# A slot dictionary in 32 bits on another queue, smaller constants, and merged weight transfers in a kernel of sliding-window attention and soft mixture of experts

## Chip, cores and metric

The kernel runs on one core of a Trainium2 chip. The metric is the time on the device in microseconds (us), lower is better; a kernel's time is the median of several runs. One run is also recorded by the hardware profiler, which gives the profile and the trace.

## What is computed

Attention over 8 batches, 8 heads, 576 positions and head size 64. Heads 0 to 3 see the last 32 positions, heads 4 to 7 every fourth of the last 128. The result, 4608 rows of 512, goes into a soft mixture of 8 experts with 4 slots each.

```python
scores = (1/8) * q @ k.T                      # per batch and head
rel = pos[:, None] - pos[None, :]
plain   = (rel >= 0) & (rel < 32)                      # heads 0-3
dilated = (rel >= 0) & (rel < 128) & (rel % 4 == 0)    # heads 4-7
attn = softmax(where(mask, scores, -1e9)) @ v
x = attn as [4608, 512]
logits = x @ phi                              # phi: [512, 32], the slot dictionary
slot_input = softmax(logits, axis=0).T @ x    # 32 slots of 512
h = relu(slot_input[e] @ w1[e])               # w1: [8, 512, 1024]
slot_out[e] = h @ w2[e]                       # w2: [8, 1024, 512]
out = softmax(logits, axis=1) @ slot_out
```

All inputs and the output are 32-bit floats; the kernel computes in 16 bits and accumulates in 32.

## The kernel before

**Engines and queues.** TensorE (PE, with its weight loads as PEld) multiplies, VectorE (DVE) and ScalarE (ACT) do elementwise work, GpSimd (POOL) does nothing but issue transfers, SyncE (SP) issues one. A transfer that POOL issues may convert 32 to 16 bits on the way, and nearly all do: q, k, v, phi and the weights come in so, and the output leaves from 16-bit tiles as 32 bits. All transfers run on the same 16 DMA engines. POOL's instructions stand in a fixed order, so a transfer that must wait holds back those behind it; those already issued queue on the DMA engines and are served in order. A transfer waits, besides its data, for the completion of an earlier one: completions are counted by eight semaphores in turn, so the ninth waits for the first.

**Loads.** For each batch `load_raw` (L184) brings Q, K and V as 128 rows of 2304 elements each, into two buffers per kind (raw). The order at the start is Q0, K0, V0, Q1, K1, phi (L459), V1; SP brings the constants `cst` (L449): the mask of the band, two masks for the last rows, an identity `ident`, a repeated small identity `spread`, and `quad`, 548 columns in all. Later `loads` (L514) brings Q, K or V of batch b + 2 as soon as batch b's buffer has been transposed, and from batch 3 on one more weight transfer with each V, the remaining early ones with the last (`load_weights`). `load_w1` brings one expert's w1 as 2 rows of 2048 per partition, `load_w2` one expert's w2 as one row of 4096. When batch 7 has been transposed (L536) the raw buffers are released, and w2_3, w2_4 and w2_5 are loaded in their place; w2_6 and w2_7 go into two slabs that held Q and K, in column halves, first the left halves of both, then the right, each half in two transfers of 4 rows of 256 (L207).

**Attention.** An order written out by hand (`ORDER`, L48) says in which sequence the steps of each batch stand and in which round each falls; it is followed literally. QT, KT and VT (L218) are transposes on VectorE out of the raw buffers. S0 to S2 (L260) are the scores in three groups, E0 to E2 (L269) their exponentials on ScalarE, MK0 to MK2 (L280) the masks on VectorE. VA to VD and their copies (L234, L240) turn V into rows with the help of `ident`. A, R and M (L303, L315, L324, L328) are products with V, reciprocals of the sums and normalisation into xp and xd. XP and XD transpose x (L344 to L351), LG multiplies it with `phi4` (L381, L389), ET (L399) keeps the exponentials, and U sums up the slots' inputs (L428, L442). `phi4` is phi four times side by side; VectorE copies it at the end of the first round (L549), between VT of batch 0 and the first mask.

**Experts.** After the last batch: row sums `rs` with `quad` (L566), the slots' inputs divided and transposed (L574 to L587), `hps` (L597) against all w1, a relu, transposes (L607), hTm (L609, L612). Then `so` (L628): one run of 32 matmuls over w2_0 to w2_3 (row chunk by row chunk, the four experts within each), eight over w2_4, eight over w2_5, then eight each over the left halves of w2_6 and w2_7. `gather_so` (L639) and `spread_so` (L644, L645, with `spread`) make so_sb of the left half, and the output of batches 0 to 5 is computed for its left columns (`emit_fin`: f L651, om L660 on ScalarE and L664 on VectorE in turn) and stored (L673), with the right halves of w2_6 and w2_7 in between; then their right columns, then batches 6 and 7 whole, then the last 64 rows of all batches (om_l, L700). The om tiles take the places of w1_0 to w1_7.

Of the kernel before, what the change touches and what calls it, by code (L numbers as in the profile page):

```python
# [19 lines left out]
WINDOW = 32  # L20
# [4 lines left out]
DMODEL = H * D  # L25
E_EXP = 8
S_PER_E = 4
N_SLOTS = 32
FDIM = 1024
# [6 lines left out]
PW = 160  # L36
LEFT = S - 512
# [24 lines left out]
def piece_w(kind, i):  # L62
    return LEFT if (kind, i) == ("P", 4) else WIDTH[kind]
# [16 lines left out]
def make_consts():  # L80

    a = np.arange(128)[:, None]
    rel = np.arange(PW)[None, :] - a
    band = (rel >= 0) & (rel < WINDOW)
    parts = [band]
    for first in LKEY:
        rel = 512 + np.arange(LEFT)[None, :] - first - a
        seen = LKEY[0] if first < LKEY[0] else S
        parts.append((rel >= 0) & (rel < WINDOW * DIL) & (rel % DIL == 0) & (first + a < seen))
    parts.append(a == np.arange(128)[None, :])  # L90
    parts.append((a % 32) == (np.arange(128)[None, :] % 32))
# [5 lines left out]
def kernel(  # L97
# [18 lines left out]
    o = PW + 2 * LEFT  # L116
    band, lmask = cst[:, 0:PW], [cst[:, PW + LEFT * i : PW + LEFT * i + LEFT] for i in range(2)]
    ident = cst[:, o : o + 128]
    spread = cst[:, o + 128 : o + 256]
    quad = cst[:, o + 256 : o + 260]  # L120
# [9 lines left out]
    so_part = consts.tile([128, DMODEL], FP16, name="so_part")  # L130
# [5 lines left out]
    w1t = [w1_pool.tile([128, 4, FDIM], FP16, name=f"w1_{e}", tag=f"w1_{e}") for e in range(E_EXP)]  # L136
    w2t = {e: w2a_pool.tile([128, 8, DMODEL], FP16, name=f"w2_{e}", tag=f"w2_{e}") for e in range(3)}


    fix = tc.alloc_tile_pool(name="fix", bufs=1)  # L140
# [50 lines left out]

    def load_w1(e):
        nc.gpsimd.dma_start(
            out=w1t[e].rearrange("p (u c) f -> p u (c f)", u=2),
            in_=moe_w1[e].rearrange("(u p c) f -> p u (c f)", u=2, p=128),
        )

    def load_w2(e, s=None):
        src = moe_w2[e].rearrange("(p c) n -> p c n", p=128)
        if s is None:  # L200
            nc.gpsimd.dma_start(
                out=w2t[e].rearrange("p c n -> p (c n)"), in_=src.rearrange("p c n -> p (c n)")
            )
            return
        cols = slice(DH * s, DH * s + DH)
        for u in range(2):
            nc.gpsimd.dma_start(out=w2t[e][:, 4 * u : 4 * u + 4, cols], in_=src[:, 4 * u : 4 * u + 4, cols])  # L207


    def turn(which, b, half):  # L210
# [245 lines left out]
    load_raw("V", 0)  # L456
    for which in "QK":
        load_raw(which, 1)
    nc.gpsimd.dma_start(  # L459
        out=phi_raw.rearrange("p (u c) s -> p u (c s)", u=2),  # L460
        in_=moe_phi.rearrange("(u p c) s -> p u (c s)", u=2, c=2),
    )
# [5 lines left out]
    weights = [(1, e) for e in range(8)] + [(2, e) for e in range(3)]  # L468

    def load_weights(n):  # L470
        for _ in range(n):
            which, e = weights.pop(0)
            (load_w1 if which == 1 else load_w2)(e)

    tmp = {}

# [49 lines left out]
    w2b_pool = None  # L526
    for it in range(B + max(s for _, s in STEPS)):
        for op, stage in STEPS:
            b = it - stage
            if not 0 <= b < B:  # L530
                continue
            step(op, b)
            if op in frees and b + 2 < B:
                loads(frees[op], b + 2)
            left.discard((op, b))
            if w2b_pool is None and not left:  # L536
                raw_pool.release()
                w2b_pool = tc.alloc_tile_pool(name="w2b", bufs=1, side="right")
                for e in (3, 4, 5):
                    w2t[e] = w2b_pool.tile([128, 8, DMODEL], FP16, name=f"w2_{e}", tag=f"w2_{e}")  # L540
                slab_weights(6, "qk0", QK_SLAB)
                slab_weights(7, "qk1", QK_SLAB)
                for e in (3, 4, 5):
# [48 lines left out]
    for fc in range(2):  # L592
        for g in range(2):
            for dc in range(4):
                for j in range(4):
                    e = 4 * g + j
# [4 lines left out]
                        start=(g == 0 and dc == 0),  # L601
                        stop=(g == 1 and dc == 3),
# [3 lines left out]
    for c in range(8):  # L606
# [34 lines left out]
    def spread_so(s):  # L641
        cols = slice(DH * s, DH * s + DH)
        rep = ring.tile([128, DH], FP32, name=f"rep_{s}", tag="ring")
        nc.tensor.matmul(rep, spread, so_part[:, cols], start=True, stop=True)  # L644
        nc.scalar.copy(out=so_sb[:, cols], in_=rep)  # L645

    turn = [0]
# [33 lines left out]
    for e in (6, 7):  # L681
        emit_so(0, (e,))
    gather_so(0)
    spread_so(0)
    for b in range(NHALF):
        if b in (2, 4):
            emit_so(1, ({2: 6, 4: 7}[b],))
        if b == 5:
            gather_so(1)
        emit_batch(b, 0, DH, 2 if b == 0 else 4)  # L690
    spread_so(1)
    for b in range(NHALF):
        emit_batch(b, DH, DMODEL)
# [45 lines left out]
```

## Time and profile before

| | us |
|---|---|
| median of 3 runs (178.29 to 178.79) | 178.5 |
| profiled execution | 178.43 |
| its span, first to last instruction | 176.7 |
| PE busy (PEld) | 123.1 (80.0) |
| DVE busy | 126.0 |
| ACT busy | 123.3 |
| POOL busy | 42.6 |

| transfers | number, size each | median from issue to landing, us |
|---|---|---|
| w, whole | 14, 1024 KB | 26.0 |
| w, halves | 8, 256 KB | 22.8 |
| Q, K, V | 24, 576 KB | 11.4 to 12.7 |
| phi | 1, 32 KB | 14.0 |
| cst | 1, 137 KB | 2.0 |
| output | 17, 256 to 1024 KB | 2.8 to 7.5 |

Sizes are those of the 16-bit side where a transfer converts into on-chip memory. The trace counts 62.07 MB read from memory and 9.44 MB written.

A profile cuts the span into 40 slices of 4.4 us and gives each engine's busy share in tenths, the granted clock of PE in tenths of full speed, the mean busy share of the 16 DMA engines, and what they moved per second, counted where it arrives. The share can pass 1 where packets overlap. A stretch (or window) gives the same between two times. A timeline row has start, duration, engine, line, operation, tiles, count, and in brackets the idle time before it and what ended it. The chain that ended last is followed back from the last instruction, at each step to what released it.

### The profile page before, as it was taken

Reading aid. Unit: us, or ns where it says so; the run is one execution under the profiler, and the core shown is the slowest. Engines: PE = TensorE matmul, PEld = TensorE weight load, DVE = VectorE, ACT = ScalarE, POOL = GpSimd, SP = SyncE. Lnnn points to the kernel's source line nnn. Section 1 sums busy time; section 2 is a strip of 40 time slices with the busy share of each in tenths; the row PEclk is TensorE's granted clock in tenths of the full one; section 3 lists DMA queues with packets and bytes.
Section 4 is the critical chain, followed back from the end, with each engine's and each line's share of the span. In section 5 each row is a group of like instructions: output and inputs, shape, how many; then the busy total and the mean of one; then the engine's idle time right before and its main releaser. Section 6 shows DMA issues by size and latency. Waiting matters only on the chain.

```text
span 176.7 us, 4735 instructions
## 1 busy us (share of the span) xinstructions
PE 123.1 (70%) x2004; PEld 80.0 (45%) x2004; DVE 126.0 (71%) x275; ACT 123.3 (70%) x266; POOL 42.6 (24%) x68
## 2 busy tenths in 40 slices
PE   0026828999888888988989888869776735769400
PEld 0015616676666666656766557646332401222000
DVE  6473999999999999999999998364131004779600
ACT  6007757999999999999999999985401104788400
POOL 7321022112112112128110013111110010765700
PEclk9999999969999999999789999996858985555555
DMA  5999999999999999999999999999999999999997
GB/s 89 210 215 209 216 213 215 214 213 215 215 214 216 214 213 215 213 213 216 213 214 214 217 211 227 209 221 217 213 213 219 192 197 174 326 400 395 402 413 222
DMA packets 19108, 40.83 MB, mean 231 GB/s; under 512 B 1296, under 2 KB 11664, under 8 KB 18320
## 3 DMA queue, kind: packets, MB, share of 16 engines
q0 software_dynamic: 18944, 40.41, 113.8%
q8 instruction: 15, 0.25, 0.5%
q1 hardware_dynamic: 144, 0.14, 0.3%
q14 instruction: 5, 0.04, 0.1%
HBM read 62.07 MB, written 9.44 MB: 405 GB/s over the span
## 4 chain that ended last, share of the span: by engine, by line
DMA 50%; DVE 27%; PE 7%; issue 5%; ACT 4%; POOL 3%; POOLq 0%
DMA w<-in_moe_w_dram 34%; DVE qk L218 10%; DMA phi_raw<-in_moe_phi_dram 8%; DMA rawQ<-in_q_dram 8%; DVE vT L218 5%; DVE p L280 5%; PE f L651 5%; ACT om L660 3%; DVE xd L328 2%; DVE xp L328 1%; PE so L628 1%; POOL rawQ L188 1%; DVE om_l L664 1%; PE s L260 1%; POOL rawV L188 1%
## 5 line engine op out<-in xcount | busy, mean ns | idle before, releaser
L269 ACT ACTIVATE p<-s 128x1920 f16<-128x1920 f32 (+1 forms) x24 | 44.2, 1840 | 10.3 <-PE s L260 10.2
L260 PE MATMUL s<-qk 32*128 32x128 f16 (+2 forms) x704 | 26.7, 295 | 18.0 <-DVE qk L218 11.9
L240 ACT COPY vX<-rv 128x768 f16<-128x768 f16 (+1 forms) x32 | 27.4, 925 | 1.8 <-PE rv L234 1.8
L303 PEld LDWEIGHTS <-p 128*128 128x128 f16 (+1 forms) x480 | 22.4, 103 | 13.7 <-DVE xp L328 4.2
L324 ACT ACTIVATE xp<-o_P,rc_P 128x64 f16<-128x64 f32 x96 | 26.1, 482 | 2.2 <-DVE rc_P L315 2.2
L260 PEld LDWEIGHTS <-qk 32*128 32x128 f16 x704 | 17.2, 117 | 21.1 <-DVE qk L218 11.9
L280 DVE TENSOR_TENSOR p<-p,masks 128x1920 f16<-128x1920 f16 (+1 forms) x24 | 25.6, 1084 | 0.0
L218 DVE STREAM_TRANSPOSE qk<-rawQ 128x576 uint32<-128x576 uint32 x16 | 18.9, 1244 | 2.6 <-DMA rawQ<-in_q_dram 2.6
L303 PE MATMUL o_P<-vX,p 128*128 128x65 f16 (+1 forms) x288 | 20.0, 205 | 0.9 <-ACT xp L324 0.2
L218 DVE STREAM_TRANSPOSE qk<-rawK 128x576 uint32<-128x576 uint32 x16 | 19.6, 1234 | 0.4 <-DMA rawK<-in_k_dram 0.4
L218 DVE STREAM_TRANSPOSE vT<-rawV 128x576 uint32<-128x576 uint32 x16 | 19.5, 1226 | 0.5 <-DMA rawV<-in_v_dram 0.5
L234 PE MATMUL rv<-cst,vT 128*128 128x128 f16 x176 | 17.6, 242 | 3.2 <-DVE vT L218 1.8
L234 PEld LDWEIGHTS <-vT 128*128 128x128 f16 x176 | 13.1, 124 | 7.6 <-issue 3.7
L664 DVE TENSOR_SCALAR om<-f,rrow 128x256 f16<-128x256 f32 (+1 forms) x28 | 13.5, 519 | 3.9 <-PE f L651 1.9
L651 PE MATMUL f<-so_sb,ET 32*128 32x256 f16 (+1 forms) x60 | 12.5, 418 | 4.1 <-ACT om L660 2.9
L660 ACT ACTIVATE om<-f,rrow 128x256 f16<-128x256 f32 (+1 forms) x28 | 12.8, 502 | 3.0 <-PE f L651 2.2
L673 POOL DMA_DIRECT2D out_dram<-om x15 | 11.1, 742 | 13.2 <-DVE om L664 8.3
L207 POOL DMA_DIRECT2D w<-in_moe_w_dram x8 | 5.9, 743 | 29.2 <-DMA w<-in_moe_w_dram 28.6
L363 ACT COPY xT<-rp 128x576 f16<-128x576 f16 x16 | 11.4, 891 | 1.2 <-PE rp L344 1.2
L188 POOL DMA_DIRECT2D rawQ<-in_q_dram x8 | 5.1, 632 | 29.2 <-DVE rc_P L315 18.4
L303 PE MATMUL o_D<-vX,p 128*128 128x65 f16 x128 | 9.9, 203 | 2.7 <-DVE xp L328 2.0
L365 ACT COPY xT<-rd 128x576 f16<-128x576 f16 x16 | 10.5, 782 | 0.1
(81 smaller groups left out, 182.9 us busy)
## 6 DMA issues: line engine op xcount, KB each, us to landing
w<-in_moe_w_dram POOLq DMA_DIRECT2D x14, 1024.0 KB, 26.0
out_dram<-om POOLq DMA_DIRECT2D x11, 512.0 KB, 4.1
rawQ<-in_q_dram POOLq DMA_DIRECT2D x8, 576.0 KB, 12.7
rawK<-in_k_dram POOLq DMA_DIRECT2D x8, 576.0 KB, 11.4
rawV<-in_v_dram POOLq DMA_DIRECT2D x8, 576.0 KB, 11.6
w<-in_moe_w_dram POOLq DMA_DIRECT2D x8, 256.0 KB, 22.8
out_dram<-om POOLq DMA_DIRECT2D x2, 1024.0 KB, 6.8
out_dram<-om_l POOLq DMA_DIRECT2D x2, 512.0 KB, 7.5
```

Of the source, the lines that this page charges most:

```text
L218: nc.vector.transpose(out=out_, in_=in_)
L234: nc.tensor.transpose(rg[:, n_t, :, c, :], rows, ident)
L240: copy(out=vX[b % 2][:, t0 : t0 + n, :, 0:D], in_=rg.rearrange("p n h c d -> p n h (c d)"))
L260: nc.tensor.matmul(sps[:, h, c0 : c0 + w], kk, qq, start=(tt == 0), stop=(tt == 1))
L269: return nc.scalar.activation(out=pt, in_=sps[:, :, 0:n], func=AF.Exp, scale=SCALE)
L280: return nc.vector.tensor_tensor(out=pt, in0=pt, in1=m, op=ALU.mult)
L303: nc.tensor.matmul(o[rows, h, :], lhs, rhs, start=(n == 0), stop=(n == len(jobs) - 1), skip_group_check=True,)
L324: nc.scalar.activation(out=dst[:, h], in_=src[:, h], func=AF.Copy, scale=rc[:, h : h + 1])
L363: copy(out=xT_t[b][:, c, :], in_=rg[:, 0:S])
L651: nc.tensor.matmul(fp[:, 0 : c1 - c0], ET[32 * j : 32 * j + 32, m : m + 128], so_sb[32 * j : 32 * j + 32, c0:c1], start=True, stop=True,)
L660: nc.scalar.activation(out=dst, in_=fp[:, 0 : c1 - c0], func=AF.Copy, scale=rrow[:, blk : blk + 1])
L664: nc.vector.tensor_scalar(out=dst, in0=fp[:, 0 : c1 - c0], scalar1=rrow[:, blk : blk + 1], scalar2=None, op0=ALU.mult)
```

## The change

- phi is kept in 32 bits (`phi_raw`) and loaded by ScalarE's hardware queue, as that engine's first instruction, instead of by POOL between K1 and V1. The copy into `phi4` converts it.
- The constants shrink from 548 columns to 290: two zero columns, the band, the two masks. `quad` is read out of the band (every 32nd column); `ident`, `fold` and `spread` are built by five VectorE operations (`build_squares`) between the first memsets and those of ET, siTm and hTm: band minus band shifted by a column, relu, two folding additions, a copy.
- Nine weight transfers become three: w1 of experts 5 to 7, w2 of experts 0 to 2, w2 of experts 3 to 5, each with a tile for three experts. Each half of w2_6 becomes one transfer of 8 rows; those of w2_7 stay two of 4. POOL issues 14 weight transfers instead of 22. The first of them are w1_0 to w1_4 with V of batches 3 to 7, as before; w1_5 to w1_7 and w2_0 to w2_2 follow the last.
- om_5 to om_7 are one tile, in the place of w1_5 to w1_7.

```diff
-    parts = [band]
+    parts = [np.zeros((128, 2)), band]
...
-    parts.append(a == np.arange(128)[None, :])
-    parts.append((a % 32) == (np.arange(128)[None, :] % 32))
-    parts.append((a // 32) == np.arange(4)[None, :])
...
+    o = 2 + PW
+    band, lmask = cst[:, 2:o], [cst[:, o + LEFT * i : o + LEFT * i + LEFT] for i in range(2)]
+    quad = band[:, WINDOW - 1 : 128 : WINDOW]
+    ident = consts.tile([128, 128], FP16, name="ident")
+    spread = consts.tile([128, 4, 32], FP16, name="spread")
+    fold = consts.tile([128, 64], FP16, name="fold")
...
-    phi_raw = consts.tile([128, 4, N_SLOTS], FP16, name="phi_raw")
+    phi_raw = consts.tile([128, 4, N_SLOTS], FP32, name="phi_raw")
...
+    EARLY = [(1, e, e + 1) for e in range(5)] + [(1, 5, 8), (2, 0, 3)]
+    early_tiles = {x: weights_tile((w1_pool, w2a_pool)[x[0] - 1], *x) for x in EARLY}
...
+    def build_squares():
+        nc.vector.tensor_tensor(out=ident, in0=cst[:, 2:130], in1=cst[:, 1:129], op=ALU.subtract)
+        nc.vector.tensor_relu(out=ident, in_=ident)
+        nc.vector.tensor_tensor(out=fold, in0=ident[:, 0:64], in1=ident[:, 64:128], op=ALU.add)
+        nc.vector.tensor_tensor(out=fold[:, 0:32], in0=fold[:, 0:32], in1=fold[:, 32:64], op=ALU.add)
+        nc.vector.tensor_copy(out=spread, in_=fold[:, None, 0:32].broadcast_to([128, 4, 32]))
...
-    def load_w1(e):
...
-    def load_w2(e, s=None):
...
+    def load_full(t, which, e0, e1):
+        if which == 1:
+            nc.gpsimd.dma_start(
+                out=t.rearrange("p e (u x) -> p (e u) x", u=2),
+                in_=moe_w1[e0:e1].rearrange("e (u p c) f -> p (e u) (c f)", u=2, p=128),
+            )
+        else:
+            nc.gpsimd.dma_start(
+                out=t, in_=moe_w2[e0:e1].rearrange("e (p c) n -> p e (c n)", p=128)
+            )
+
+    def load_half(e, s, n):
         src = moe_w2[e].rearrange("(p c) n -> p c n", p=128)
...
+        for u in range(0, 8, n):
+            nc.gpsimd.dma_start(out=w2t[e][:, u : u + n, cols], in_=src[:, u : u + n, cols])
...
     nc.sync.dma_start(out=cst, in_=consts_dram.ap())
+    nc.scalar.dma_start(
+        out=phi_raw.rearrange("p (u c) s -> p u (c s)", u=2),
+        in_=moe_phi.rearrange("(u p c) s -> p u (c s)", u=2, c=2),
+    )
...
-    nc.gpsimd.dma_start(
-        out=phi_raw.rearrange("p (u c) s -> p u (c s)", u=2),
-        in_=moe_phi.rearrange("(u p c) s -> p u (c s)", u=2, c=2),
-    )
     load_raw("V", 1)
     build_masks()
+    build_squares()
...
-                for e in (3, 4, 5):
-                    load_w2(e)
+                load_full(late, 2, 3, 6)
                 for s in range(2):
                     for e in (6, 7):
-                        load_w2(e, s)
+                        load_half(e, s, 8 if e == 6 else 4)
...
-    om = [w1_pool.tile([128, 4, DMODEL], FP16, name=f"om_{b}", tag=f"w1_{b}") for b in range(B)]
+    om = [w1_pool.tile([128, 4, DMODEL], FP16, name=f"om_{b}", tag=f"w1_{b}") for b in range(5)]
+    om567 = w1_pool.tile([128, 3, 4, DMODEL], FP16, name="om_5", tag="w1_5")
+    om += [om567[:, i] for i in range(3)]
```

More of the change, by code (lines that the diff above doesn't have):

```diff
@@ L115 @@
     cst = consts.tile([128, consts_np.shape[1]], FP16, name="cst")
[L116 to L120, printed above, removed]
+    o = 2 + PW
[4 more added lines that the diff above has]
+    fold = consts.tile([128, 64], FP16, name="fold")
     masks = consts.tile([128, NMASK], FP16, name="masks")
-    phi_raw = consts.tile([128, 4, N_SLOTS], FP16, name="phi_raw")
+    phi_raw = consts.tile([128, 4, N_SLOTS], FP32, name="phi_raw")
     phi4 = consts.tile([128, 4, 4, N_SLOTS], FP16, name="phi4")
@@ L135, with weights_tile @@
     w2a_pool = ctx.enter_context(tc.tile_pool(name="w2a", bufs=1))
-    w1t = [w1_pool.tile([128, 4, FDIM], FP16, name=f"w1_{e}", tag=f"w1_{e}") for e in range(E_EXP)]
-    w2t = {e: w2a_pool.tile([128, 8, DMODEL], FP16, name=f"w2_{e}", tag=f"w2_{e}") for e in range(3)}
+    w1t, w2t = {}, {}
+    def weights_tile(pool, which, e0, e1):
+        n = (4 * FDIM, 8 * DMODEL)[which - 1]
+        t = pool.tile([128, e1 - e0, n], FP16, name=f"w{which}_{e0}", tag=f"w{which}_{e0}")
+        for e in range(e0, e1):
+            of = t[:, e - e0]
+            if which == 1:
+                w1t[e] = of.rearrange("p (c f) -> p c f", c=4)
+            else:
+                w2t[e] = of.rearrange("p (c n) -> p c n", c=8)
+        return t
+    EARLY = [(1, e, e + 1) for e in range(5)] + [(1, 5, 8), (2, 0, 3)]
+    early_tiles = {x: weights_tile((w1_pool, w2a_pool)[x[0] - 1], *x) for x in EARLY}
     fix = tc.alloc_tile_pool(name="fix", bufs=1)
@@ L190, in load_raw @@
         )
-    def load_w1(e):
-        nc.gpsimd.dma_start(
-            out=w1t[e].rearrange("p (u c) f -> p u (c f)", u=2),
-            in_=moe_w1[e].rearrange("(u p c) f -> p u (c f)", u=2, p=128),
-        )
-    def load_w2(e, s=None):
-        src = moe_w2[e].rearrange("(p c) n -> p c n", p=128)
[L200 to L204, printed above, removed]
+    def load_full(t, which, e0, e1):
+        if which == 1:
+            nc.gpsimd.dma_start(
+                out=t.rearrange("p e (u x) -> p (e u) x", u=2),
+                in_=moe_w1[e0:e1].rearrange("e (u p c) f -> p (e u) (c f)", u=2, p=128),
+            )
+        else:
+            nc.gpsimd.dma_start(
+                out=t, in_=moe_w2[e0:e1].rearrange("e (p c) n -> p e (c n)", p=128)
+            )
+    def load_half(e, s, n):
+        src = moe_w2[e].rearrange("(p c) n -> p c n", p=128)
         cols = slice(DH * s, DH * s + DH)
-        for u in range(2):
-            nc.gpsimd.dma_start(out=w2t[e][:, 4 * u : 4 * u + 4, cols], in_=src[:, 4 * u : 4 * u + 4, cols])
+        for u in range(0, 8, n):
+            nc.gpsimd.dma_start(out=w2t[e][:, u : u + n, cols], in_=src[:, u : u + n, cols])
     def turn(which, b, half):
@@ L458 @@
         load_raw(which, 1)
-    nc.gpsimd.dma_start(
-        out=phi_raw.rearrange("p (u c) s -> p u (c s)", u=2),
-        in_=moe_phi.rearrange("(u p c) s -> p u (c s)", u=2, c=2),
-    )
     load_raw("V", 1)
     build_masks()
+    build_squares()
     nc.vector.memset(ET, 0.0)
@@ L467 @@
     nc.vector.memset(hTm, 0.0)
-    weights = [(1, e) for e in range(8)] + [(2, e) for e in range(3)]
+    weights = list(EARLY)
     def load_weights(n):
         for _ in range(n):
-            which, e = weights.pop(0)
-            (load_w1 if which == 1 else load_w2)(e)
+            x = weights.pop(0)
+            load_full(early_tiles[x], *x)
     tmp = {}
@@ L538 @@
                 w2b_pool = tc.alloc_tile_pool(name="w2b", bufs=1, side="right")
-                for e in (3, 4, 5):
-                    w2t[e] = w2b_pool.tile([128, 8, DMODEL], FP16, name=f"w2_{e}", tag=f"w2_{e}")
+                late = weights_tile(w2b_pool, 2, 3, 6)
                 slab_weights(6, "qk0", QK_SLAB)
                 slab_weights(7, "qk1", QK_SLAB)
-                for e in (3, 4, 5):
-                    load_w2(e)
+                load_full(late, 2, 3, 6)
                 for s in range(2):
                     for e in (6, 7):
-                        load_w2(e, s)
+                        load_half(e, s, 8 if e == 6 else 4)
         if it == 0:
@@ L643, in spread_so @@
         rep = ring.tile([128, DH], FP32, name=f"rep_{s}", tag="ring")
-        nc.tensor.matmul(rep, spread, so_part[:, cols], start=True, stop=True)
+        nc.tensor.matmul(rep, spread.rearrange("p a i -> p (a i)"), so_part[:, cols], start=True, stop=True)
         nc.scalar.copy(out=so_sb[:, cols], in_=rep)
```

## The prediction

> **What bounds the kernel now.** I read the slices of the page first, then its DMA queues, then the chain that ended last, then stretches and engine timelines where the change touches them.
>
> ```profile
> PEclk9999999969999999999789999996858985555555
> DMA  5999999999999999999999999999999999999997
> GB/s 89 210 215 209 216 213 215 214 213 215 215 214 216 214 213 215 213 213 216 213 214 214 217 211 227 209 221 217 213 213 219 192 197 174 326 400 395 402 413 222
> ...
> q0 software_dynamic: 18944, 40.41, 113.8%
> q8 instruction: 15, 0.25, 0.5%
> q1 hardware_dynamic: 144, 0.14, 0.3%
> ...
> DMA 50%; DVE 27%; PE 7%; issue 5%; ACT 4%; POOL 3%; POOLq 0%
> ```
>
> From the second slice to the last but one the DMA engines are never idle. Up to slice 30 they write about 214 GB/s (casting loads read twice what they write), then 192 to 197 while the halves of w2_6 and w2_7 arrive, then about 400 while the output leaves. VectorE and ScalarE are as full from 30 to 110 us, but transfers queue far ahead of them: the last ones are issued at 105 to 141 us. DVE's 27% of the chain is how the walk back happened to go; had DVE been faster, the queue would have held the same bytes. So the end is: first bytes, all loads, the hand-over from loads to stores, all stores.
>
> The hand-over, as stretches (start and end; busy PE, PEld, DVE, ACT, POOL with counts; granted clock, DMA share, GB/s), then PE's timeline (start, duration, group, idle before it and who ended it):
>
> ```profile
> 147.00:148.00 1.00, 0.37 (x1) 0.10 (x1) 0.30 (x1) 0.23 (x1) 0.00 (x0) 0.50 1.46 197
> 149.00:150.00 1.00, 0.88 (x8) 0.39 (x11) 0.94 (x3) 0.91 (x4) 0.26 (x1) 0.50 0.94 127
> 150.00:151.00 1.00, 0.92 (x12) 0.25 (x13) 0.58 (x3) 0.47 (x2) 1.00 (x2) 0.50 0.63 86
> 151.00:152.00 1.00, 0.58 (x4) 0.25 (x3) 0.93 (x3) 0.91 (x3) 0.91 (x2) 0.50 1.82 366
> ```
> ```profile
> 129.86 5.59 PE L597 MATMUL hps<-w,siTm 128*32 128x512 f16 x64 [0.28 <-DVE siTm L587]
> ...
> 138.17 2.34 PE L628 MATMUL so<-w,hTm 128*32 128x512 f16 x40 [0.52 <-DVE hTm L609]
> 141.07 0.62 PE L628 MATMUL so<-w,hTm 128*32 128x512 f16 x8 [0.56 <-DMA w<-in_moe_w_dram]
> 142.41 0.29 PE L628 MATMUL so<-w,hTm 128*32 128x256 f16 x4 [0.73 <-DMA w<-in_moe_w_dram]
> 143.93 0.29 PE L628 MATMUL so<-w,hTm 128*32 128x256 f16 x4 [1.22 <-DMA w<-in_moe_w_dram]
> 145.13 0.41 PE L628 MATMUL so<-w,hTm 128*32 128x256 f16 x4 [0.91 <-DMA w<-in_moe_w_dram]
> 146.43 0.41 PE L628 MATMUL so<-w,hTm 128*32 128x256 f16 x4 [0.89 <-DMA w<-in_moe_w_dram]
> ```
>
> Two things meet at 151. The engines run out of loads one after another (197, 127, 86 GB/s), the slowest near 151; and the half of w2_7 that lands at 146.4 goes through so, so_part, rep, so_sb, f and om to the first store, issued by POOL at 149.74, whose bytes flow from 151. After that 9.44 MB at about 400 GB/s is 23.6 us: 174.6, and the last engine stops between 174 and 175. Whatever brings 146.4 and 151 forward together brings the end forward by as much.
>
> **The change, part by part.**
>
> *phi off POOL's queue.* It lies there between K1 and V1. Its cost, from quarter stretches:
>
> ```profile
> 17.00:17.25 0.25, 0.25 (x5) 0.25 (x4) 0.00 (x0) 0.25 (x1) 0.00 (x0) 1.00 0.89 105
> 17.25:17.50 0.25, 0.25 (x5) 0.25 (x3) 0.00 (x0) 0.25 (x1) 0.00 (x0) 1.00 2.00 226
> 17.50:17.75 0.25, 0.25 (x4) 0.15 (x2) 0.00 (x0) 0.25 (x1) 0.00 (x0) 1.00 1.54 262
> 17.75:18.00 0.25, 0.17 (x2) 0.14 (x1) 0.00 (x0) 0.25 (x1) 0.00 (x0) 1.00 0.90 184
> ```
>
> These move 0.25 x (105+226+262+184) = 194 KB, 33 KB of them phi. The other 161 KB take 0.75 us at 214 GB/s, so phi cost 0.25 us of every engine. Saved: **-0.25**.
>
> *phi and smaller constants at the start.* The hardware queues then carry 128 rows of 580 bytes (74 KB) and 256 pieces of 256 bytes (66 KB), the bytes of the 140 KB now. The constants run from about 1.7 to 2.3 us, before Q0's first bytes near 2.5, and the engines are half idle until 3.75 (share 0.55 in 3.0 to 3.5). Phi's 256 pieces at the 0.25 above plus half of today's 0.55 end at 2.25: no loss. At the page's 0.3% of 16 x 176.7 us over 144 packets, 59 ns each, 384 packets on 16 engines last 1.4 us, to 3.1, and Q0 loses 0.6. Range 0 to +0.6; I take **+0.1**, nearer phi's own row. ScalarE's issue (0.34 us on SP now) stands ahead of the table load and six mask copies, which end at 4.23 and are first needed at 18.
>
> *Five VectorE operations* build ident, fold and spread. Nearest rows: 0.10 (a 128x44 memset) to 0.23 (er, 128x160), so 0.5 to 1.15 us together. They wait for the constants (landed by 2.78 now), and the memsets of ET, siTm and hTm (2.1 us) queue behind them: done by 2.78+1.15+2.1 = 6.0, while VectorE idles until Q0 at 6.75. Cost 0; without that cover at most 1.15, of VectorE's time only. The first transposes that need ident run at 14.7.
>
> *VectorE's 3.4 us wait for phi at L549 goes.* It goes straight on to mask and Q1 (landed near 15), some 3 us ahead; what is late next is K1, near 17.8. The copy reads 32 bits: 0.29 now, at most the 0.75 of a 128x512 from PSUM. Raw loads are then issued up to 3 us earlier, into a queue that is already full: 0 at the end.
>
> *Merging.* Eight weight transfers fewer on POOL (22 to 14), so eight completions fewer on each engine. All descriptors keep their size and order of experts. Five w2 landings that free POOL at 112.58 to 136.50 are 4.78 us apart for 1.05 MB, 219 GB/s; raw loads with a completion every 0.59 MB run at 215. If completions made all of that difference, one costs 2.743 - 2.693 = 0.05. Range 0 to -0.4; phi's whole transfer cost 0.25 with 256 pieces, so one completion is nearer the low end, 0.025: **-0.2**. The Trainium skill (DMA: Bandwidth & Descriptors, "Anatomy of one DMA") gives about 2 us of fixed cost to each transfer and elsewhere advises merging. The halves land 1.2 to 1.5 us apart in PE's rows, so that cost overlaps here; charged in full, an estimate from that page would be eight times 2 us, 16 less.
>
> *What merging makes late.* w2_3, 4 and 5 now land as one, where w2_5 landed, 141.07. PE's fourth `so` matmul needs w2_3 and stands in front of all others, so the 40 that ran from 138.17 queue up with the eight of w2_5. Until 146.4 they have 5.4 us. At clock 1.0 twelve groups of four take 12 x 0.234 = 2.8. But PE, some 3 us ahead, will then have waited from about 135, and the clock fell to 0.5 at 144.05, 2.4 us after the last dense group: count on half clock. There `hps` ran four matmuls per 0.427 us, so twelve groups are 5.1, w2_6 0.43 and w2_7's first 0.21: 146.8, and w2_7's second group ends 147.24 instead of 146.84, **+0.4**. `hps` however got clock 1.0 after 4.0 us (129.86 to 133.9). With that, 9.4 groups are done at 145.07 and the rest, at full clock, by 146.0: no delay, and the chain up to the first store runs some 0.3 faster, which helps little as the slowest engine still has loads. Range -0.3 to +0.4, taken **0**. The Trainium skill (TensorE: Matmul & The Clock Gate, Part 1) says that the array falls to half clock after an idle window of about 3.4 us and recovers after a busy one; the drop at 144.05 and the recovery at 133.9 agree. It speaks against the merged wait: by it alone the sum would be 0 to 0.4 worse.
>
> *w2_6's halves as 8 rows, one tile for om_5 to om_7:* the first w2_6 group waits one landing longer (1.3 us before w2_7's first), the second adds no wait in the built order. 0.
>
> Sum: -0.25 + 0.1 - 0.2 = -0.35. The profiled execution took 178.43 (span 176.7 plus 1.7 around it), so 178.08; the median 178.5 lies 0.07 above it: **178.1**.
>
> **The rivals.** What a measurement here can tell from no change is 0.3%, 0.54 us: faster is below 177.96, slower above 179.04.
>
> A, the forecast, 178.1, own range 177.7 to 178.5. For it: DMA never idle. Chance 0.43, of which 0.13 faster.
>
> B, all ends good: phi 0.25, completions 0.4, start 0, and the warm clock's 0.3 in full: 177.55. For it, PE's recovery row; against, the slowest engine's own loads. 0.22, faster.
>
> C, PE late at half clock (+0.4, and merging worth nothing): 178.5 - 0.25 + 0.1 + 0.4 = 178.75. It decides if the clock has not returned by about 146. 0.10, of which 0.03 slower.
>
> D, **the other side**: one DMA engine falls further behind. Fetches of instructions are 15 packets taking 0.5% of 16 x 176.7 us, 0.94 each, and one engine pays each; the ragged end from 148 to 151 fits engines that paid unequally. If moved timing puts one more on the slowest, every store waits for it: 178.1 + 0.94 = 179.05. It decides once that engine ends loads after the first store's bytes could flow. Against: PE's instructions are as many as before. 0.15, of which 0.12 slower.
>
> E, the start collides: +0.6 instead of +0.1, 178.6. 0.05, of which 0.02 slower.
>
> F, merging and moving are hidden altogether: 178.5, same. 0.04.
>
> G, a transfer holds the queue for a fixed time, the most that the halves' 1.34 us between landings allow: eight times that, 167.4. Against: 1.05 MB lands in 4.78, at the full rate. 0.01, faster. The Trainium skill's figure above would make it 162.
>
> Faster 0.13+0.22+0.01 = 0.36; slower 0.03+0.12+0.02 = 0.17, which I raise to 0.20 for effects that no row shows; the rest, 0.44, is no change. Range 177.4 (B and a little) to 179.1 (D).
>
> **What would show it.** Right: no dip near 17 us; VectorE at mask 0 near 15; `so` in one run from about 140.7, at clock 0.5 first; w2_7's first half landing near 146.0; first store bytes near 150.6; 9.44 MB at 400 GB/s as before. Wrong: Q0 landing after 6.75 (E); PE still busy when w2_7 lands (C); loads ending later than 151 (D); any DMA slice below 0.9 in mid-run, since all of this rests on a full queue.

## The result, and the profile after

The changed kernel takes 178.62 us (median of 22 runs, 178.36 to 179.15), the kernel before 178.47 in the 22 runs beside it (178.14 to 178.79). The ratio of the runs is 1.0018, 95% interval 1.0012 to 1.0024, so by the ratio the change costs 0.2 to 0.4 us where 0.35 of gain was forecast (the medians differ by 0.15, the means by 0.26). The profiled execution took 178.81, its span 177.0 (before: 178.43 and 176.7).

First the slices, the queues and the chain's shares on the page of the changed kernel:

```profile
PEclk9999999999999999999999999996788558555555
DMA  5999999999999999999999999999999999999997
GB/s 87 204 217 214 216 208 212 218 214 215 213 215 218 212 212 215 217 213 210 216 216 215 213 219 220 217 211 222 217 209 224 189 198 160 318 399 395 402 412 217
...
q0 software_dynamic: 18544, 40.37, 113.3%
q8 instruction: 15, 0.25, 0.5%
q1 hardware_dynamic: 144, 0.07, 0.2%
q10 hardware_dynamic: 272, 0.07, 0.2%
...
DMA 36%; DVE 18%; ACT 17%; PE 13%; issue 8%; POOL 1%; POOLq 0%; ACTq 0%
```

The picture is that of before: the DMA engines are busy in every slice but the first and the last, 214 GB/s and then 400. q0 has 400 packets fewer (phi's 256, and 16 for each of nine completions), q10 is phi on ScalarE's queue. The loss can't be seen on this page.

Quarter stretches where phi's dip lay before:

```profile
17.00:17.25 0.25, 0.25 (x4) 0.25 (x5) 0.25 (x1) 0.25 (x1) 0.00 (x0) 1.00 0.66 129
17.25:17.50 0.25, 0.25 (x5) 0.25 (x4) 0.25 (x2) 0.25 (x1) 0.00 (x0) 1.00 1.02 203
17.50:17.75 0.25, 0.25 (x6) 0.25 (x4) 0.25 (x2) 0.25 (x1) 0.00 (x0) 1.00 1.37 277
17.75:18.00 0.25, 0.25 (x5) 0.25 (x4) 0.25 (x1) 0.25 (x1) 0.00 (x0) 1.00 1.27 258
```

217 KB instead of 194, and VectorE is at work instead of waiting. The timeline of the start (start, duration, group, idle before it and its releaser):

```profile
2.70 0.23 DVE L182 TENSOR_TENSOR ident<-cst 128x128 f16<-128x128 f16 x1 [0.94 <-DMA cst<-consts_d]
...
7.23 2.34 DVE L236 STREAM_TRANSPOSE qk<-rawQ 128x576 uint32<-128x576 uint32 x2 [0.90 <-DMA rawQ<-in_q_dram]
...
14.97 0.41 DVE L566 CAST phi<-phi_raw 128x512 f16<-128x512 f32 x1
```

VectorE passes phi and reaches mask 0 near 15, as forecast. But Q0 was turned at 6.75 before, and is turned at 7.23 here. Then PE's timeline at the end of the loads, and the granted clock there (last but two of a stretch's figures):

```profile
126.79 4.89 PE L614 MATMUL hps<-w,siTm 128*32 128x512 f16 x64 [0.28 <-DVE siTm L604]
...
134.40 0.40 PE L647 MATMUL so<-w,hTm 128*32 128x512 f16 x3 [0.52 <-DVE hTm L626]
141.35 5.68 PE L647 MATMUL so<-w,hTm 128*32 128x512 f16 x61 [6.56 <-DMA w<-in_moe_w_dram]
```
```profile
142.00:143.00 1.00, 1.00 (x12) 0.37 (x8) 0.00 (x0) 0.00 (x0) 0.00 (x0) 0.50 1.45 197
...
146.00:147.00 1.00, 1.00 (x21) 0.69 (x14) 0.00 (x0) 0.00 (x0) 0.00 (x0) 0.78 1.48 194
147.00:148.00 1.00, 0.30 (x2) 0.15 (x2) 0.42 (x1) 0.14 (x1) 0.00 (x0) 1.00 1.46 198
```

`hps` comes 3 us sooner, `so` runs as one piece from 141.35, at half clock into the stretch from 146 to 147, and the chain behind it, up to om's first pieces, at full clock, where before had 0.50. From 150 the changed kernel is at 0.50 again. The last link, from om's first pieces to the store, in the timelines of before, of the changed kernel and of the changed kernel with four small POOL instructions more (e5 below):

```profile
148.69 1.43 DVE L664 TENSOR_SCALAR om<-f,rrow 128x256 f16<-128x256 f32 x3 [1.38 <-DMA w<-in_moe_w_dram]
...
149.74 0.70 POOL L673 DMA_DIRECT2D out_dram<-om  x1 [7.68 <-DVE om L664]
```
```profile
148.68 1.72 DVE L683 TENSOR_SCALAR om<-f,rrow 128x256 f16<-128x256 f32 x4 [1.18 <-DMA w<-in_moe_w_dram]
...
150.07 2.91 POOL L692 DMA_DIRECT2D out_dram<-om  x4 [37.02 <-DVE om L683]
```
```profile
148.41 1.72 DVE L686 TENSOR_SCALAR om<-f,rrow 128x256 f16<-128x256 f32 x4 [1.18 <-PE f L673]
...
149.47 3.04 POOL L695 DMA_DIRECT2D out_dram<-om  x4 [35.40 <-DVE om L686]
```

From the start of om to the store: 1.05, 1.39, 1.06 us. The changed kernel had om ready when before had it, and issued its store 0.33 later.

**What sets the end.** The trace holds, for each transfer, the moments at which its 16 DMA engines reported it done; whoever waits for the transfer waits for the last of them. (The Trainium skill says the same: DMA: Bandwidth & Descriptors, "Why a DMA increments its semaphore by 16 and not by 1".) The kept trace does not say which engine reported, so the slowest of one transfer need not be the slowest of the next. The table has the middle and the slowest engine for V1 and for the last load (w2_7's last), the end of om's first piece and the issue of the first store, all in us from POOL's first issue, so that the start of an execution drops out, and the span:

```
                            V1            last load       om      store   span
                            mid    slow   mid     slow    ready   issued
before                      19.31  19.55  149.09  150.47  147.90  148.47  176.66
e1_before_again             19.31  19.82  148.90  150.85  148.27  148.84  177.04
e8_consts_only              19.27  19.61  149.01  150.54  147.97  148.54  176.73
e14_consts_again            19.32  19.56  149.16  150.46  147.89  148.45  176.68
e3_merges_only              19.35  19.80  148.82  150.71  147.83  148.39  176.81
e9_merges_consts            19.23  19.60  148.83  150.38  147.51  148.07  176.48
e13_merges_consts_again     19.25  19.46  148.82  150.09  147.23  147.79  176.20
e7_phi_only                 19.19  20.18  148.79  151.15  148.58  149.15  177.38
e2_phi_consts_only          19.13  19.59  148.96  150.52  147.95  148.52  176.77
changed                     19.13  19.77  148.66  150.54  147.88  148.79  177.04
e6_changed_again            19.26  19.67  148.77  150.44  147.57  148.48  176.72
e4_late_three_split         19.11  19.73  148.65  150.51  148.01  148.56  176.77
e5_pool_shift               19.17  19.73  148.71  150.48  147.62  148.18  176.61
e16_pool_shift_again        19.22  19.83  148.82  150.61  147.74  148.30  176.73
e10_phi_after_masks         19.49  19.61  149.16  150.30  147.98  148.88  177.13
e11_phi_on_sp               19.05  19.67  148.57  150.44  147.57  148.48  176.72
e12_phi_after_masks_shift   19.44  20.39  149.40  150.23  147.91  148.48  176.76
e15_no_phi_shift            19.04  19.20  148.71  149.99  147.47  148.03  176.28
```

All 18 spans follow from two columns within 0.06 us: span = 2.59 + the later of (store issued + 25.63) and (slowest engine's last load + 23.52). The three constants are fitted to these spans; e13 to e16 were run after the constants were on record. Before: 148.47 + 25.63 = 174.10 against 150.47 + 23.52 = 173.99, so 176.69 (176.66). The two limits stand 0.1 apart: an earlier store alone gains 0.1 at most. Single profiles of one kernel differ by up to 0.4 (before and e1), so small effects are read from the timed runs.

### The profile page after: what moved, and what is told of

Read it like the earlier page. It is cut to its first block, busy times and chain, and to the rows that moved or that the text cites. A ratio compares the mean times of both kernels' runs of the same rounds, so it can differ in the third digit from the quotient of the medians.

```text
span 177.0 us, 4730 instructions
## 1 busy us (share of the span) xinstructions
PE 120.8 (68%) x2004; PEld 79.5 (45%) x2004; DVE 127.2 (72%) x280; ACT 123.1 (70%) x266; POOL 37.7 (21%) x59
## 4 chain that ended last, share of the span: by engine, by line
DMA 36%; DVE 18%; ACT 17%; PE 13%; issue 8%; POOL 1%; POOLq 0%; ACTq 0%
DMA w<-in_moe_w_dram 22%; DMA rawV<-in_v_dram 14%; DVE vT L236 5%; DVE qk L236 5%; PE f L670 5%; ACT p L287 5%; PE so L647 4%; ACT om L679 3%; DVE p L298 3%; ACT vX L258 3%; ACT xp L342 2%; PE s L278 2%; PE rv L252 2%; ACT xT L381 1%; DVE xd L346 1%
## 5 line engine op out<-in xcount | busy, mean ns | idle before, releaser
L287 ACT ACTIVATE p<-s 128x1920 f16<-128x1920 f32 (+1 forms) x24 | 45.5, 1895 | 10.3 <-PE s L278 10.2
L258 ACT COPY vX<-rv 128x768 f16<-128x768 f16 (+1 forms) x32 | 28.7, 981 | 1.7 <-PE rv L252 1.7
L342 ACT ACTIVATE xp<-o_P,rc_P 128x64 f16<-128x64 f32 x96 | 27.6, 545 | 0.0
L278 PEld LDWEIGHTS <-qk 32*128 32x128 f16 x704 | 17.7, 117 | 20.7 <-DVE qk L236 12.4
L321 PEld LDWEIGHTS <-p 128*128 128x128 f16 (+1 forms) x480 | 21.5, 100 | 11.8 <-issue 3.6
L321 PE MATMUL o_P<-vX,p 128*128 128x65 f16 (+1 forms) x288 | 19.4, 201 | 1.0 <-DVE xd L346 0.3
L252 PE MATMUL rv<-ident,vT 128*128 128x128 f16 x176 | 17.5, 243 | 2.8 <-DVE vT L236 1.8
L381 ACT COPY xT<-rp 128x576 f16<-128x576 f16 x16 | 11.9, 955 | 1.0 <-PE rp L362 1.0
L647 PE MATMUL so<-w,hTm 128*32 128x512 f16 (+1 forms) x80 | 7.3, 514 | 7.1 <-DMA w<-in_moe_w_dram 6.6
L383 ACT COPY xT<-rd 128x576 f16<-128x576 f16 x16 | 11.0, 850 | 0.2 <-PE rd L369 0.2
```

The source lines that it names most:

```text
L252: nc.tensor.transpose(rg[:, n_t, :, c, :], rows, ident)
L258: copy(out=vX[b % 2][:, t0 : t0 + n, :, 0:D], in_=rg.rearrange("p n h c d -> p n h (c d)"))
L278: nc.tensor.matmul(sps[:, h, c0 : c0 + w], kk, qq, start=(tt == 0), stop=(tt == 1))
L287: return nc.scalar.activation(out=pt, in_=sps[:, :, 0:n], func=AF.Exp, scale=SCALE)
L321: nc.tensor.matmul(o[rows, h, :], lhs, rhs, start=(n == 0), stop=(n == len(jobs) - 1), skip_group_check=True,)
L342: nc.scalar.activation(out=dst[:, h], in_=src[:, h], func=AF.Copy, scale=rc[:, h : h + 1])
```

## The experiments

Times are medians, ratios are to the kernel before on the same chip, with 95% intervals. Before took 178.44 beside e1 to e4, 178.41 beside e5 to e8, 178.32 beside e9 to e12 and 178.35 beside e13 to e16.

**The parts.** e1 is the kernel before once more.

> The kernel before once more, to see what repeats. In the two profiles the VectorE part of the first om tile ends at 149.17 (before) and 149.13 (changed), but POOL issues the first store at 149.74 and 150.04: 0.56 and 0.91 later. Theory S (POOL, idle for 37 us in the changed kernel and for 8 in the one before, starts its first store late): here 0.56 again, within 0.05, and a span of 176.7. Theory D (what counts is the slowest DMA engine, and which engines pay for fetches of instructions is fixed by the program): the landing of w2_5 on the slowest engine again near 141.0 and about 2.65 us after the first engine; if fetches fall at random, that spread moves by 0.3 or more.

178.46, 1.0003 (0.9991 to 1.0014): what no change looks like, though its one profile has a span of 177.0.

e2 has phi and the small constants, with all 22 weight transfers as before.

```diff
-    EARLY = [(1, e, e + 1) for e in range(5)] + [(1, 5, 8), (2, 0, 3)]
+    EARLY = [(1, e, e + 1) for e in range(8)] + [(2, e, e + 1) for e in range(3)]
...
-                load_full(late, 2, 3, 6)
+                for e in (3, 4, 5):
+                    load_full(late[:, e - 3 : e - 2], 2, e, e + 1)
...
-                        load_half(e, s, 8 if e == 6 else 4)
+                        load_half(e, s, 4)
```

> Phi in 32 bits on ScalarE's queue and the small constants, all weight transfers as before (22). Theory S: POOL's halves are issued up to 141 again, so the first store is issued 0.56 after om, and the time is that of the kernel before or better: 178.2 to 178.5. Theory P (the merged wait of w2_3 to w2_5 makes PE late, and that alone costs): the same, 178.2 to 178.5, and PE's so waits for each landing as before. Theory D, with the start as its main cost (Q0's last engine landed 0.4 us later in the changed kernel): Q0 is first transposed at 7.2 instead of 6.75, and half or all of the 0.25 saved on phi is lost on the slowest engine: 178.4 to 178.7.

178.66, 1.0011 (1.0002 to 1.0020): slower without any merging, and with the store 0.56 behind om.

e3 has the merged weights alone; constants, phi and their queues are those of before.

> All merges (14 weight transfers), phi and constants as before. Theory S: POOL's last weight transfer is issued near 115, it idles some 35 us, the first store comes 0.9 after om: 178.7 to 178.9. Theory P: PE starts its 48 so matmuls at 141 and ends w2_7's first half 0.2 to 0.4 later, the store late by that: 178.7 to 178.9, but with 0.56 between om and store. Theory D: Q0 at 6.75, completions saved 0.2 on the median engine: 178.2 to 178.5.

178.26, 0.9994 (0.9983 to 1.0005). POOL had been idle for 34 us before the store (37 in the changed kernel), and the store still came 0.56 behind om: the idleness is not what delays it.

e4 is the changed kernel with w2_3, 4 and 5 in three transfers (the second hunk of e2).

> The changed kernel with w2_3, w2_4, w2_5 in three transfers again; the rest stays merged (16 weight transfers). Theory P: PE's so runs in pieces as before, w2_7's first half is multiplied right on landing, the time falls by 0.2 to 0.4 against the changed kernel, to 178.2 to 178.4. Theory S: POOL issues its last half when w2_3 has landed, near 131, and idles 18 instead of 37; if the late issue is a matter of idling, the gap between om and store lies between 0.56 and 0.91, and the time 178.3 to 178.6. Theory D: 178.6, as the changed kernel.

178.53, 1.0004 (0.9996 to 1.0012). The link from w2_7's landing to om's first piece is 2.78, as in before, against 2.47 in the repeat of the changed kernel (e6), where the granted clock there is 1.0 instead of 0.50: that is what the merged wait saves. In exchange the store comes 0.56 behind om instead of 0.91.

**The late store.** The trace's packets of queue 14 (instructions) are 8 KB, five within each span, 0.32 us each as a rule. In all 18 profiles the first and the third come when VectorE has started about 52 and 180 instructions, the second and the fourth when ScalarE has started about 71 and 197, so these go with those two engines; the fifth goes with POOL. Before has it at 110.9, while POOL waits; the changed kernel has it at 150.3, taking 0.47. So e5 adds four POOL instructions early on, which moves POOL's boundary.

```diff
+    idle = consts.tile([128, 4], FP16, name="idle")
...
     load_raw("V", 1)
+    for i in range(4):
+        nc.gpsimd.memset(idle[:, i : i + 1], 0.0)
     build_masks()
```

> The changed kernel with four tiny memsets more on POOL behind V1's issue, of a tile that nothing reads. In the changed kernel's profile a fetch of 8 KB of instructions stands at 150.26, just where POOL starts its first store 0.35 late (0.91 instead of 0.56 after om); in no other profile so far is there a fetch near that place, and there the gap is 0.56 to 0.57, also after 35 us of idling (merges only). Theory S2 (POOL's instruction fetch falls between its wait and the first store, by the place of the store in POOL's program): the four instructions move the fetch before the wait, the gap is 0.56, the time 0.2 to 0.35 below that of the changed kernel: 178.3 to 178.45. Theory C (that gap was chance): gap 0.56 here and in the repeat of the changed kernel, and both at 178.6.

178.42, 1.0004 (0.9993 to 1.0016). POOL's fetch is at 114.3, the other four are where they were, and the store is 0.57 behind om.

> The changed kernel once more. Theory S2: gap 0.9 and a fetch near 150 again, 178.6. Theory C: gap 0.56 and no fetch there, 178.6.

178.62, 1.0012 (1.0000 to 1.0023); fetch at 150.0, store 0.91 behind om: the place of the fetch belongs to the program, not to chance. Merging without phi's move (e3, e9, e13: 116 to 119) and phi's move without merging (e2, e7: 116) leave it in POOL's wait; together they put it at the store.

**Phi.** e7 is the kernel before with nothing but phi moved: 32 bits, on ScalarE's queue, beside constants of full size.

```diff
-    phi_raw = consts.tile([128, 4, N_SLOTS], FP16, name="phi_raw")
+    phi_raw = consts.tile([128, 4, N_SLOTS], FP32, name="phi_raw")
...
     nc.sync.dma_start(out=cst, in_=consts_dram.ap())
+    nc.scalar.dma_start(
+        out=phi_raw.rearrange("p (u c) s -> p u (c s)", u=2),
+        in_=moe_phi.rearrange("(u p c) s -> p u (c s)", u=2, c=2),
+    )
...
-    nc.gpsimd.dma_start(
-        out=phi_raw.rearrange("p (u c) s -> p u (c s)", u=2),
-        in_=moe_phi.rearrange("(u p c) s -> p u (c s)", u=2, c=2),
-    )
```

> The kernel before with phi in 32 bits on ScalarE's queue, and nothing else. Phi with the small constants alone took 178.66 against 178.44 before. Theory D1 (phi's 256 pieces delay the start of one engine by what the queue saves; net 0): 178.4 to 178.5, V1 on the slowest engine 19.7 us after POOL's first issue as before, on the median engine 19.1 instead of 19.3. Theory D2 (phi on the hardware queue costs more than it saves): 178.6 to 178.7. By the forecast's terms (-0.25 and +0.1): 178.3.

179.06, 1.0034 (1.0022 to 1.0046), the worst of all. V1's middle engine gains 0.12, its slowest loses 0.63 (19.55 to 20.18). The timeline of e7 has Q0 turned at 7.62:

```profile
7.62 2.34 DVE L218 STREAM_TRANSPOSE qk<-rawQ 128x576 uint32<-128x576 uint32 x2 [3.46 <-DMA rawQ<-in_q_dram]
```

e8 has the small constants and the five VectorE operations alone; e14 is the same again.

> The kernel before with the small constants and the five VectorE operations, phi on POOL in 16 bits. Forecast: nothing, 178.4 to 178.5. Rival D3 (the cost of 0.2 that phi and constants have together lies here, for instance in PE's moving reads or in VectorE): 178.6 to 178.7.

> The kernel before with small constants built by five VectorE operations, once more. Its first profile had the slowest engine's loads and the store where before has them. Theory: no gain, 178.4 or so, within 0.1 of before; if the smaller constants are worth 0.2 as first timed: 178.2.

178.20, 0.9990 (0.9980 to 1.0000), and 178.26, 0.9997 (0.9988 to 1.0006): no loss, perhaps 0.1 of gain. In the profiles the store and the slowest engine stand where they stand in before, so a gain is not shown.

e9 is the changed kernel with phi as it was before (16 bits, POOL's queue); e13 is the same again.

```diff
-    phi_raw = consts.tile([128, 4, N_SLOTS], FP32, name="phi_raw")
+    phi_raw = consts.tile([128, 4, N_SLOTS], FP16, name="phi_raw")
...
-    nc.scalar.dma_start(
+    nc.gpsimd.dma_start(
```

(the transfer itself stands between K1 and V1 again)

> The changed kernel with phi as it was (16 bits, POOL's queue, between K1 and V1); merged weights and small constants stay. Theory (the loss lies in phi's transfer beside the start: merges and small constants are worth 0.2 us each, phi on ScalarE's queue costs 0.45): 178.0 to 178.1 with the store 0.56 us behind om, 178.3 if a fetch of instructions stands there. Rival (phi off POOL's queue is worth 0.25 as forecast, and the loss has another source): 0.25 slower than the changed kernel, 178.85.

> The kernel with merged weights and small constants, phi in 16 bits on POOL's queue, once more. In the profiles so far the end is the later of two: the first store's issue + 25.63, and the slowest engine's last load + 23.52 (both from POOL's first issue, span 2.59 behind). Theory: merging helps the store by 0.32 but the slowest engine's loads by 0.1 to 0.15 alone, so 0.1 to 0.2 faster than before: 178.2 to 178.35. If the parts simply add up (merges 0.15, constants 0.2): 178.05.

178.29, 0.9996 (0.9985 to 1.0007), and 178.23, 0.9994 (0.9985 to 1.0003). It is faster than the changed kernel, and can't be told from the kernel before. The parts do not simply add up: in both profiles the store is early enough (148.07, 147.79) that the slowest engine's loads set the end.

e10 moves phi's issue behind ScalarE's six mask copies, e11 onto SP's queue behind the constants, e12 is e10 with e5's four memsets.

```diff
     build_masks()
+    nc.scalar.dma_start(
+        out=phi_raw.rearrange("p (u c) s -> p u (c s)", u=2),
+        in_=moe_phi.rearrange("(u p c) s -> p u (c s)", u=2, c=2),
+    )
     build_squares()
```

> The changed kernel with phi's issue behind ScalarE's six mask copies, at about 4.3 us, when Q0's bytes are under way. POOL's instructions are the changed kernel's, so the store should again be 0.91 us behind om. Theory (phi costs by standing between the constants and Q0's first bytes): Q0's slowest engine lands near its median again and V1's slowest 0.2 us sooner after POOL's first issue (19.5, changed 19.7); time 178.3. Rival (256 short pieces cost the engine that is last as much wherever they are): 178.6, as the changed kernel.

> The changed kernel with phi on SP's queue, behind the constants, 0.05 us or so later and without a second hardware queue. If the two hardware queues side by side make the one engine late: 178.3. If it is phi's 256 pieces ahead of Q0, on whichever queue: 178.6 or more. If it is ScalarE's issue ahead of its table load: 178.2, with ScalarE's first copy earlier by 0.4 us.

> As the run with phi behind the mask copies, with the four small POOL memsets besides (a tile that nothing reads). Theory: both causes gone, the store 0.56 us behind om; 178.0 to 178.1. Rival (phi's place does not matter): 178.4, as the changed kernel with the four memsets.

178.83, 1.0018 (1.0009 to 1.0028); 178.66, 1.0021 (1.0012 to 1.0029); 178.31, 1.0000 (0.9991 to 1.0010). My theory of the place is not borne out: neither the later place nor the other queue is shown to help. In e10 phi's packets lie among Q0, K0 and V0 from 6.5 to 12.6 us; V1's slowest engine has then caught up (19.61), but the middle one has lost (19.49). In e12, with phi at the same place, three engines bring V1 at 20.3 to 20.4, and still the last load ends early (150.23). In e10 and e11 the store is 0.91 behind om again, with a fetch at 150.4 and 150.0; with the four memsets (e12) the fetch is at 113.7, the store 0.56 behind om. On one chip, e10 to e12 is 0.5 us between medians, with intervals that just touch; the two limits account for 0.4 of it.

e15 leaves phi's transfer out altogether; e16 is e5 again, beside it.

```diff
-    nc.scalar.dma_start(
-        out=phi_raw.rearrange("p (u c) s -> p u (c s)", u=2),
-        in_=moe_phi.rearrange("(u p c) s -> p u (c s)", u=2, c=2),
-    )
+    nc.vector.memset(phi_raw, 0.03)
```

> The changed kernel with the four small POOL memsets (no fetch ahead of the store) and with phi's transfer left out altogether, a VectorE memset in its place (the output is not the reference's). If phi's 256 short pieces on the hardware queue make an engine late: V1's slowest 0.2 to 0.3 us sooner after POOL's first issue (19.45), and 0.2 to 0.3 us under the same kernel with phi, 178.15. If phi costs nothing there and the saving goes to waste on the slowest engine for another reason: 178.4, the same as with phi.

> The changed kernel with the four small POOL memsets once more, for the run without phi to be held against on the same chip: store 0.56 us behind om, the slowest engine's last load + 23.52 as the end, 178.4.

178.14, 0.9984 (0.9973 to 0.9995), against 178.41, 1.0009 (1.0000 to 1.0018), intervals that do not meet. Without phi V1's slowest engine is at 19.20, 0.16 behind the middle one; with it 19.83, 0.61 behind. Q0 in the timelines of e15 and e16:

```profile
6.67 1.26 DVE L237 STREAM_TRANSPOSE qk<-rawQ 128x576 uint32<-128x576 uint32 x1 [0.56 <-DMA rawQ<-in_q_dram]
```
```profile
7.29 2.34 DVE L237 STREAM_TRANSPOSE qk<-rawQ 128x576 uint32<-128x576 uint32 x2 [0.95 <-DMA rawQ<-in_q_dram]
```

## Why the prediction was wrong, point by point

**phi off POOL's queue (-0.25) and the start (+0.1).** This is the step that failed. Both numbers were right for an engine in the middle: in the seven profiles with phi on POOL's queue V1's middle engine is at 19.23 to 19.35, in the eight with it on a hardware queue at the start at 19.05 to 19.26, 0.13 less on average for the -0.15 forecast, and without any phi 19.04, the 0.25 of the quarter stretches. But the step said "of every engine", and the slowest engine saved nothing: 19.46 to 19.82 with phi on POOL's queue, 19.59 to 19.83 on a hardware queue (20.18 in e7). Q0's landing, w2_7's landing and the last load all count by whichever engine is last, so the net is not -0.15. The timed runs, all without the late store, put it at +0.2 to +0.3: e5 and e16 (1.0004, 1.0009) against e9 and e13 (0.9996, 0.9994), and without merging e2 (1.0011) against e8 and e14 (0.9990, 0.9997). The term that was mis-sized is the start: with e15 as the kernel without phi, e16 puts phi's transfer on the hardware queue at 0.3 (medians) to 0.4 (ratios) for the +0.1, while 0.2 lies between e15 and the two with phi on POOL's queue (e9, e13; intervals overlap), near the 0.25.

That the late engines at V1 are the way by which phi costs at the end is argued, not shown. In e7 and e12 V1's slowest engine is about equally late (20.18, 20.39), but the last load ends at 151.15 in e7 and at 150.23 in e12. Rival E, the start, had the mechanism and its sign to look for, Q0 after 6.75 (7.23); its price, 0.6, was worked out for all 16 engines together, while only some are late: in the changed kernel four bring Q0 0.3 to 0.6 after the middle one, in e11 one.

**POOL's instructions: no term.** The working counted completions, and had nothing for where POOL's instructions fall. The changed kernel's count puts an instruction fetch at the first store: 0.91 instead of 0.56 in the four profiles with the fetch at 150 (changed, e6, e10, e11), and 0.56 to 0.57 in the fourteen without. By the two limits that costs 0.35 of the span in changed and e10 and 0.15 in e6 and e11, where the slowest engine's loads come next. Taking it away was worth 0.2 between medians (e6 to e5, intervals overlap) and 0.5 (e10 to e12). No rival had it; D looked for a fetch on a DMA engine, not for the engine that waits for its instructions. The Trainium skill (Runtime: NRT & Kernel Launch, "Instruction fetch mechanics") says that an engine fetches ahead while it works and that a block's boundary is mostly hidden: in the fourteen profiles POOL's fetch falls elsewhere and no delay of the store is seen, in the four it shows with 0.35.

**Merging (-0.2).** Right for the middle engine, not shown for the time: e3 is 0.9994, 0.1 faster, with an interval from 0.3 faster to 0.1 slower that holds both 0 and the forecast. The middle engine's last load is 0.2 sooner (148.82 in e3 against 149.04, the mean of before, e1, e8 and e14), the slowest's is not (150.71 against 150.58).

**The merged wait at half clock (0, -0.3 to +0.4).** The granted clock fell and came back as described; full clock was there by 147 at the latest, and the link to om shrank from 2.79 to 2.47 (2.66 in the first profile, where PE still had 0.6 us of work when w2_7 landed). Rival C, PE late, lengthened the link by 0.2 there and by 0.5 in e15, where the loads land sooner and the link is 2.95; in the other profiles with the merged wait, by nothing. The sentence that the 0.3 "helps little as the slowest engine still has loads" held: with the store early the second limit, + 23.52, takes over in e3, e5, e9, e13 and e16.

**Five VectorE operations, phi's wait, w2_6 and om (0).** Right. They run from 2.70 to 3.92, the memsets end at 6.33, Q0 is later; VectorE runs 3 us ahead, and nothing comes of it. Smaller constants were counted at nothing. Beside phi on POOL's queue 0.1 of gain is possible, not shown (e8, e14); beside phi on ScalarE's queue they are worth 0.4, with intervals that do not meet (e7 1.0034, e2 1.0011).

**The signs to look for.** No dip at 17, mask 0 near 15, `so` from 141.35 at 0.5, 400 GB/s: as forecast. w2_7's half landed at 146.5 for 146.0, and the store came late: its bytes flow from about 151.3 for 150.6. Loads end later than 151 (151.8), but that sign tells nothing: by its semaphore before's slowest engine ends them at 151.7, which the stretches did not show. The sum from the runs is -0.1 (merging and constants together, e9 and e13) + 0.2 (phi) + 0.2 (fetch) = about +0.3, within the measured 0.2 to 0.4, though the interval of each term is about as wide as the term.

Not settled: why 256 pieces of 256 bytes on a hardware queue leave some DMA engines behind and 256 pieces on POOL's queue do not. ScalarE's own queue is not the whole cause (e11). What the hardware queues carry ahead of Q0 goes with it: Q0's slowest engine is 0.1 to 0.3 us behind its middle one with the small constants alone (e8, e9, e13, e14, e15), 0.2 to 0.5 with the large ones (before, e1, e3), 0.3 to 0.6 with the small ones and phi (changed, e2, e4, e5, e6, e11, e16) and 1.0 with the large ones and phi (e7). With phi later it is 0.2 in e10 but 1.0 in e12, so chance or another cause has a part.

## What to carry to other kernels

Where a wait is for a transfer over 16 DMA engines, cost an edit on the slowest engine, not on the mean: a saving in a full queue can be lost if the edit makes some engines late by as much. Where two limits end within 0.1 us of each other, price both before counting a gain on either. And when the number of instructions on an engine changes, look where its instruction fetches fall: one at the instruction that everything waits for cost here what a small optimisation brings, and four harmless instructions moved it.

## What the runs showed that was not expected

- POOL fetches 8 KB of instructions once within each span, in 0.32 us as a rule, and in fourteen profiles this falls into a wait. At the first store it goes with 0.35 us of delay of the store, always at the same place in the same program. That the store waits for it is inferred: the packet is recorded 0.2 us after the store's own start, and the two come and go together in 18 profiles.
- 64 KB of phi on a hardware queue at the start, 0.16% of the kernel's bytes, left the slowest DMA engine 0.4 to 1.0 us behind the middle one for V1, against 0.2 to 0.5 with phi on POOL's queue and 0.16 without phi. In e7 (1.0, four engines) the whole kernel is 0.6 us slower; in e12, with phi later, three engines were 0.8 to 0.9 behind, and the time is that of the kernel before (1.0000).
- The 16 engines drift apart by themselves: before has 0.5 us between its first and last engine at V1 (20.36 to 20.82 in span time) and 2.7 at the last load (149.09 to 151.74). Instruction fetches of 16 KB, 15 packets of about 0.9 us, would fit that size if they fell unequally on the engines; it was not tried.
